# Products of weights and keys on four 32-column tiles of the array, and a new plan of the first loads

## The chip, the cores and the metric

The kernel runs on one core of a Trainium2 chip. The metric is the device time of one execution in microseconds (us); the median of several runs is compared. The core's engines are called PE (TensorE), DVE (VectorE), ACT (ScalarE), POOL (GpSimd) and SP (SyncE, which only issues transfers here).

## What is computed

Two layers, each a Fourier mixing step and a product-key mixture of experts, both with a residual:

```python
def _A_ref(x, dft_seq_re, dft_seq_im, dft_hid_re, dft_hid_im):
    a = jnp.einsum("bsd,ed->bse", x, dft_hid_re)
    b = jnp.einsum("bsd,ed->bse", x, dft_hid_im)
    return jnp.einsum("ts,bse->bte", dft_seq_re, a) - jnp.einsum("ts,bse->bte", dft_seq_im, b)

def _B_ref(x, w_q, k1, k2, u, v):          # S=2048, D=512, H=32, dk=128, E=16, K=2
    q = jnp.einsum("nd,dhc->nhc", xf, w_q)
    q1, q2 = q[..., :dk], q[..., dk:]
    s1 = jnp.einsum("nhd,ed->nhe", q1, k1)
    s2 = jnp.einsum("nhd,ed->nhe", q2, k2)
    ...  # the best 2 of each, the best 2 of their 4 sums, softmax g, experts ue and ve
    act = _gelu(jnp.einsum("nd,nhkd->nhk", xf, ue))
    return jnp.einsum("nhk,nhk,nhkd->nd", g, act, ve)

x = x + _A_ref(_layernorm(x), ...)
x = x + _B_ref(_layernorm(x), ...)
x = x + _A_ref(_layernorm(x), ...)
x = x + _B_ref(_layernorm(x), ...)
```

## The kernel before

Tokens lie in 16 row tiles `rows[:, r]` of 128 tokens by 512. The scores of a token are its row times `w_q` times the keys, so the kernel multiplies `w_q` by the keys once, at the start, and keeps the product in two f16 words, `wh` and `wl`. It also uses the symmetries of the Fourier matrices: rows that mirror each other are added and subtracted first ("folded").

The work ahead of the first row of scores is this:

- **Rows of x** (`load_x`): 7 by SP, 9 gathered by POOL. Each gets statistics on DVE (`ln_bn`), one power on POOL and a scaling on ACT.
- **Folds** (`fold`, four of them, q = 0 to 3, each of four row tiles): about ten additions of 512 columns on DVE, with small steps on POOL; the result is `eo` in two words.
- **Fourier blocks** (`load_c`, `load_edges`, and `dhid` in `setup`): loads, then splits on ACT and DVE into `cc`, `edge`, `tcol` and `dd`.
- **Weights times keys** (`setup`, `visit(f, g)`): for each of the two key matrices f and four groups g of eight heads, 2 MB of `w_q` come in four loads of 512 KB into four buffers of `wraw` (pool "wr"). `kpad` holds the 16 keys eight times along a diagonal in zeros, so that a 128-column weight of it puts head z's scores into output rows 16 z to 16 z + 15; eight f32 products of 512 columns (L1867) add up in one bank. ACT copies the bank (L1877), PE transposes it in four pieces (L1882), ACT and DVE split it into `wh` and `wl`.
- **Experts' tables**: `ut` and `vm`, split into `uh`, `ul`, `vh`, `vl`.
- **Mixing along the sequence** (`seq_pair`, L1941): `eo` times `cc`, pair by pair, then `hidden` (L2072), which adds to the rows.

Then `peers` runs for each of 16 rows in each of two layers, and `L2154` is its first product, the scores: it waits for all of `setup_done`, which holds every split of `w_q`, `ut` and `vm`. Beside the rows runs a check of the Fourier matrices' symmetry, on ACT, DVE, POOL and by loads into the buffers `raws` (pool "raw", six of 512 KB).

The order on every engine is set when the kernel is built. Each piece of work is an `op` with an engine, an assumed time, what it waits for, the buffers it takes and gives back, and a priority `prio`. `Plan.best` lays them out in time twice, the second time by due times worked out from the first, and the instructions are issued in that order. For a load the assumed time is a tuple (issue, transfer, latency), and not more than `LANES` = 8 may be under way on a queue. At issue, PE also gets products that nothing reads (`fill`, L2710) wherever the plan has it idle.

Of the kernel before, what the change touches and what calls it, by code (L numbers as in the profile page):

```python
# [17 lines left out]
P = 128  # L18
# [11 lines left out]
E = 16  # L30
# [189 lines left out]
def load(kb):  # L220
    return 0.5, kb / 256 * 0.98, 2.05
# [1175 lines left out]

class Late:
# [22 lines left out]
REPOSE, STEP = 0.25, 0.065  # L1421
EARLY = 2


@with_exitstack
def folded(ctx: ExitStack, tc, flag, x_in, cseq, ctile, dhid, wq, k1t, k2t, ut, vm, out):
# [57 lines left out]
    kpad = [spare[:, f * 1152:(f + 1) * 1152] for f in range(2)]  # L1484
# [32 lines left out]
    nc.vector.memset(spare[:, :2304], 0.0)  # L1517
# [28 lines left out]
    slots = {"wr": [0, 1, 2, 3], "ws": [0, 1], "code": [0, 1, 2], "pq": [0, 1]}  # L1546
# [73 lines left out]
    def load_x(r, turn):  # L1620
# [6 lines left out]
        xload[r] = op("SP" if place(r) else "POOL", load(256), f, prio=(-2, turn))  # L1627
        xstat[0, r] = ln_bn(lambda: rows[:, r], stats[0][:, r], FS, [xload[r]], (-4, r // 4, 0, r))
# [102 lines left out]
    def load_c(n, c, prio, low):  # L1731
# [7 lines left out]
        a = op("SP", load(512), f, take=[h], prio=low)  # L1739
# [18 lines left out]
    def load_edges():  # L1758
        h, one_ = Hold("raw"), {}

        def f0():
            for z, (n, c) in enumerate(((6, 0), (6, 1))):
                for h in range(2):
                    nc.sync.dma_start(tc32[:, z, 2 * h:2 * h + 2], cseq[n, c, 2 * h:2 * h + 2, :, 0].rearrange("i p -> (i p)").rearrange("(p a) -> p a", a=2))

        def f1():
            for p in (0, 32, 64):
                nc.sync.dma_start(one_[0][p:p + 1], cseq[0:2, 0, 4, 0:1, :].rearrange("n p t -> p n t"))
                nc.sync.dma_start(one15[p:p + 1], cseq[6, 0, 4, 0:1, 0:1])
# [28 lines left out]
        b = op("ACT", 0.6, g2, [b], prio=(-3, 20))  # L1798
# [4 lines left out]
    def setup():  # L1803
# [29 lines left out]
        a = op("SP", load(512), f, take=[hd, hd2], prio=(-1, 0))  # L1833
        b = op("SP", (0.5, 0.2, 2.0), f_mid, behind=[a], prio=(-1, 1))
# [5 lines left out]
        for f, kt in enumerate((k1t, k2t)):  # L1840
# [933 lines left out]
```

## Time and profile before

| | |
|---|---|
| Median of 3 runs | 660.16 us (659.52 to 660.43) |
| Profiled execution | 664.53 us, span 662.5 us |
| PE, busy | 559.7 us, 84% of the span |
| DVE, busy | 504.6 us, 76% |
| ACT, busy | 394.6 us, 60% |
| POOL, busy | 242.2 us, 37% |
| Granted clock of PE, mean | 0.949 |
| Moved by DMA | 88.29 MB, mean 133 GB/s |

All times in the profile are from one profiled execution, counted from its span's start. A row of the timeline has start, length, engine, line, operation, output <- input, tile of the array, shape and count; in brackets stands the idle time ahead of it and what ended it. SPq and POOLq rows are the issuing of transfers, not their moving. "issue" means that the engine waited for nothing that the profile shows.

### The profile page before, as it was taken

The numbers are of one execution on the slowest core, as the hardware profiler recorded it, in microseconds if no ns is written. First come the engines' busy times: TensorE is split into PE (matmuls) and PEld (weight loads), VectorE is DVE, ScalarE is ACT, GpSimd is POOL, SyncE is SP. The second block draws the span as 40 slices with busy tenths as digits, with TensorE's granted clock in tenths as the row PEclk, the third lists the DMA queues.
The fourth block names the chain that finished last, engine by engine and source line by source line (L and its number), as shares of the span: only waits on it lengthen the run. The fifth ranks groups of instructions, "written<-read, shape, count | busy, mean of one in ns | idle before, by whom it ended". The sixth has DMA issues, their size and how long they took to land.

```text
span 662.5 us, 17484 instructions
## 1 busy us (share of the span) xinstructions
PE 559.7 (84%) x7083; PEld 363.4 (55%) x7115; DVE 504.6 (76%) x1001; ACT 394.6 (60%) x995; POOL 242.2 (37%) x370
## 2 busy tenths in 40 slices
PE   3986899998978879888995758998979988999965
PEld 2644455654555646446554647655656555555553
DVE  3579823797798878899598434689994899889963
ACT  2148326996668866857655625947863865554450
POOL 7254000355156627315145100331723263431730
PEclk9997999998999979989997986999989999999988
DMA  8785573439656687573729230044798569795683
GB/s 306 211 294 176 162 253 128 140 57 182 96 157 119 108 183 113 97 128 49 145 49 144 31 133 1 1 97 94 106 194 144 120 101 223 137 178 130 116 169 57
DMA packets 174702, 88.29 MB, mean 133 GB/s; under 512 B 138758, under 2 KB 151570, under 8 KB 174614
## 3 DMA queue, kind: packets, MB, share of 16 engines
q1 hardware_dynamic: 161718, 52.49, 34.5%
q0 software_dynamic: 12896, 34.61, 27.4%
q8 instruction: 57, 0.93, 0.6%
q14 instruction: 31, 0.25, 0.1%
HBM read 78.68 MB, written 8.39 MB: 131 GB/s over the span
## 4 chain that ended last, share of the span: by engine, by line
PE 37%; DVE 36%; DMA 8%; ACT 8%; issue 5%; POOL 3%; SPq 2%; another core or an unknown queue 0%; POOLq 0%; DVEq 0%; ACTq 0%
PE sc L2154 13%; DVE eq L2200 6%; DVE val L2195 6%; PE bank L1867 6%; DMA gt<-gdr 5%; PE bank L2384 3%; DVE wraw L2307 3%; DVE wraw L2312 3%; PE bank L2168 3%; PE bank L2328 2%; DMA gdr<-spare 2%; PE small L2710 2%; PE small L2208 2%; PE bank L2072 2%; SPq L2345 1%
## 5 line engine op out<-in xcount | busy, mean ns | idle before, releaser
L2154 PE MATMUL sc<-wh,xt 128*128 128x512 f16 x512 | 132.9, 386 | 0.7
L2154 PEld LDWEIGHTS <-xt 128*128 128x128 f16 x768 | 74.2, 99 | 84.5 <-issue 4.7
L1597 POOL TENSOR_TENSOR stats<-stats,half 128x1 f32<-128x1 f32 x48 | 32.5, 677 | 197.9 <-ACT stats L1594 197.9
L2195 DVE TENSOR_REDUCE val<-sc 128x64 f32<-128x1024 f32 x64 | 77.8, 1218 | 22.8 <-PE sc L2154 14.8
L2444 POOL DMA_DIRECT2D raws<-in_cseq x56 | 59.0, 1080 | 56.2 <-issue 38.3
L2200 DVE TENSOR_TENSOR eq<-sc,val 128x1024 bf16<-128x1024 f32 x64 | 77.8, 1217 | 0.7
L2415 ACT ACTIVATE raws<-raws 128x1024 f32<-128x1024 f32 (+2 forms) x68 | 68.7, 1011 | 10.0 <-DVE raws L2420 7.0
L2710 PE MATMUL small<-ident 128*128 128x64 f16 x1272 | 52.6, 202 | 20.4 <-DVE small L1548 6.5
L2154 PE MATMUL sc<-wl,xt 128*128 128x512 f16 x256 | 66.9, 384 | 0.0
L2710 PEld LDWEIGHTS <-ident 128*128 128x128 f16 x1272 | 49.0, 104 | 29.9 <-issue 22.1
L1867 PE MATMUL bank<-wraw,spare 128*128 128x512 f32 x128 | 61.4, 626 | 0.0
L2334 ACT ACTIVATE spare<-bank 128x512 f32<-128x512 f32 x64 | 36.7, 595 | 32.8 <-PE bank L2328 30.7
L2208 PE MATMUL small<-eq,power 128*128 128x64 bf16 x1024 | 41.9, 196 | 16.3 <-DVE eq L2200 12.7
L2208 PEld LDWEIGHTS <-power 128*128 128x128 bf16 x1024 | 38.5, 100 | 22.4 <-issue 14.3
L2328 PE MATMUL bank<-wraw 64*64 64x64 f16 x2048 | 43.7, 198 | 7.9 <-DVE wraw L2312 2.8
L2328 PEld LDWEIGHTS <-wraw 64*64 64x64 f16 x2048 | 39.2, 114 | 19.9 <-issue 16.5
L2307 DVE TENSOR_TENSOR wraw<-places,qt 128x2048 f16<-128x2048 f16 x32 | 41.5, 1295 | 8.8 <-ACT qt L2290 8.8
L2312 DVE TENSOR_TENSOR wraw<-wraw,qt 128x1024 f16<-128x1024 f16 x64 | 43.7, 693 | 0.3
L2384 PE MATMUL bank<-vh,pp 128*128 128x512 f16 x128 | 41.3, 406 | 3.1 <-DVE pp L2371 3.0
L2168 PEld LDWEIGHTS <-xt 128*128 128x128 f16 x384 | 36.9, 98 | 9.4 <-issue 1.5
L1591 ACT ACTIVATE junk<-rows 128x512 f16<-128x512 f32 x48 | 30.0, 626 | 19.3 <-DVE rows L2388 12.0
L2168 PE MATMUL bank<-uh,xt 128*128 128x256 f16 x256 | 39.0, 276 | 1.6 <-ACT pd L1987 0.7
(235 smaller groups left out, 1108.9 us busy)
## 6 DMA issues: line engine op xcount, KB each, us to landing
raws<-in_cseq POOLq DMA_DIRECT2D x40, 512.0 KB
wraw<-in_wq SPq DMA_DIRECT2D x32, 512.0 KB
raws<-in_cseq SPq DMA_DIRECT2D x32, 512.0 KB
gdr<-spare SPq DMA_DIRECT2D x128, 32.0 KB
gt<-gdr SPq DMA_DIRECT2D x64, 64.0 KB
raws<-in_ctile SPq DMA_DIRECT2D x32, 128.0 KB
raws<-in_cseq POOLq DMA_DIRECT2D x16, 256.0 KB
rows<-in_x SPq DMA_DIRECT2D x7, 256.0 KB
```

What stands on the lines that cost most here:

```text
L1867: nc.tensor.matmul(t["b"], kpad[f][:, z * P:(z + 1) * P], t["wr", m][:, a], start=(z == 0), stop=(z == 7))
L2154: nc.tensor.matmul(t["sc"][:, f], t["x"][:, z, k], m[:, k, f], start=(n == 0), stop=False, skip_group_check=True)
L2168: nc.tensor.matmul(t["xu"], t["x"][:, z, k], m[:, k], start=(n == 0), stop=(n == 3 * KD - 1))
L2195: nc.vector.tensor_reduce(t["val"][:, k], flip(), axis=AX.X, op=ALU.max)
L2200: nc.vector.tensor_tensor(t["eq"], t["sc"], t["val"][:, k][:, :, None, :].to_broadcast([P, 2, E, H]), op=ALU.is_equal)
L2208: nc.tensor.matmul(t["code", k], power[:, e], t["eq"][:, :, e], start=(e == 0), stop=(e == E - 1), skip_group_check=True)
L2307: nc.vector.tensor_tensor(t["m"][:, 0:2].rearrange("p v g e t -> p (v g) e t"), io, both, op=ALU.is_equal)
L2312: nc.vector.tensor_mul(t["m"][:, 2 + k], t["m"][:, 1], row_of(2 + k))
L2328: nc.tensor.matmul(pg[js, g], t["m"][js, 0, 8 * z + g], t["m"][js, 2 + k, 8 * z + g], start=(k == 0), stop=(k == 1), skip_group_check=True)
L2384: nc.tensor.matmul(t["po"], t["pp"][:, z, k], m[:, k], start=(n == 0), stop=(n == 5))
L2415: nc.scalar.activation((to or src)(), src(), AF.Square, accum_out=sq[:src().shape[0], k:k + 1])
L2710: nc.tensor.matmul(small[:, 448:], ident16, ident16[:, :64], start=False, stop=True, skip_group_check=True)
```

## The change

The product of weights and keys now uses 32-column tiles of the array. `kpad` shrinks to 64 columns per key matrix: two weights of 32 columns, the keys in the first 16 columns of one and the last 16 of the other. A piece of `w_q` is four heads of equal parity by half of the columns (256), still 512 KB, in runs of 1 KB instead of 2 KB. Its four products go to output rows 32 j to 32 j + 31 for j = 0 to 3, each on column tile j; two pieces (even and odd heads) add up.

Nine of the 32 pieces (the 15th and every second one after it, counted from 0) take a buffer of `raws`, so that there are ten buffers in all. All loads of the first stage get a new assumed time, 0.70 us for 256 KB instead of 0.98, and new priorities; several small loads that were one `op` become one `op` each. The plan issues no fills before its time 45.

```diff
+def fetch(kb):
+    return 0.5, kb / 256 * 0.70, 2.05
...
+COLD = 45.0
+SHARED = range(15, 32, 2)
+def ORDER(k):
+    return 0.75 * k + WFIRST
+WFIRST = 10
...
-    kpad = [spare[:, f * 1152:(f + 1) * 1152] for f in range(2)]
+    kpad = [spare[:, f * 64:(f + 1) * 64] for f in range(2)]
...
-    nc.vector.memset(spare[:, :2304], 0.0)
+    nc.vector.memset(spare[:, :128], 0.0)
...
-        a = op("SP", (2.0, 1.7, 2.0, 4), f0, prio=(-2, 15, 4))
+        a = [op("SP", (0.5, 0.4, 2.0), f0(z, h), prio=(-2, 14.3, 1)) for z in range(2) for h in range(2)]
...
-        b = op("SP", (3.0, 0.2, 2.0, 6), f1, [b], prio=(-2, 15, 5))
+        b = [op("SP", (0.5, 0.05, 2.0), f1(p, z), [b], prio=(-2, 14.3, 2)) for p in (0, 32, 64) for z in range(2)]
...
-        a = op("SP", load(512), f, take=[hd, hd2], prio=(-1, 0))
+        a = op("SP", fetch(512), f, take=[hd, hd2], prio=(-2, 14.4))
...
-                diagonal = kpad[f].rearrange("p (h x) -> p h x", x=P + E)[:, :, :E]
-                nc.vector.tensor_copy(diagonal, kr[:, f][:, None, :].to_broadcast([P, 8, E]))
+                for a in range(2):
+                    nc.vector.tensor_copy(kpad[f][:, 3 * E * a:3 * E * a + E], kr[:, f])
...
-            for m in range(4):
-                h = Hold("wr")
+            for z in range(4):
+                k = 16 * f + 4 * g + z
+                h = Hold("raw" if k in SHARED else "wr")
...
-                    nc.sync.dma_start(t["wr", m], wq[f, 8 * g + 2 * m:8 * g + 2 * m + 2].rearrange("h c d -> c h d"))
+                    nc.sync.dma_start(t["w", z], wq[f, 8 * g + z % 2:8 * g + 8:2, :, z // 2 * T:(z // 2 + 1) * T].rearrange("h c d -> c h d"))
...
-                    for a in range(2):
-                        z = 2 * m + a
-                        nc.tensor.matmul(t["b"], kpad[f][:, z * P:(z + 1) * P], t["wr", m][:, a], start=(z == 0), stop=(z == 7))
+                    a, d = z % 2, z // 2 * T
+                    for j in range(4):
+                        nc.tensor.matmul(t["b"][32 * j:32 * j + 32, d:d + T], kpad[f][:, 32 * a:32 * a + 32], t["w", z][:, j], start=(a == 0),
+                                         stop=(a == 1), skip_group_check=True, tile_position=(0, 32 * j))
...
-                a_pe = op("PE", 2 * 0.87, f1, [a, kready[f], a_pe], take=[] if m else [hb], last=[h], prio=(-1, f, g))
+                o = op("SP", fetch(512), f0, take=[h], prio=(-2, ORDER(k)))
+                a_pe = op("PE", 0.55, f1, [o, kready[f], a_pe], take=[] if z else [hb], last=[h], prio=(-1, f, g))
...
-            a = op("SP", load(512), f0, take=[h], prio=(-1, 3, z))
+            a = op("SP", fetch(512), f0, take=[h], prio=(-2, ORDER(27), z))
...
-    idle = 0.0
+    idle = COLD
...
-            idle = o.start + o.us
+            idle = max(idle, o.start + o.us)
```

Since the plan is made anew, the order changes on every engine. Lines move too: the product L1867 becomes L1881, the sequence products L1941 become L1954, the first scores product L2154 becomes L2167, the `w_q` load L1860 becomes L1874.

SP, from the kernel's start, before (rows of x are L1623, cseq blocks L1736):

```order
L1842 DMA kr<-in_k1t 128x16
L1842 DMA kr<-in_k2t 128x16
L1860 DMA wraw<-in_wq 128x2x512 x4
L1623 DMA rows<-in_x 128x512 x3
L1736 DMA raws<-in_cseq 128x2x512 x2
L1860 DMA wraw<-in_wq 128x2x512 x4
L1623 DMA rows<-in_x 128x512 x4
```

and now (rows of x are L1635, cseq blocks L1751):

```order
L1635 DMA rows<-in_x 128x512
L1874 DMA wraw<-in_wq 128x4x256
L1856 DMA kr<-in_k1t 128x16
L1874 DMA wraw<-in_wq 128x4x256
L1635 DMA rows<-in_x 128x512
L1874 DMA wraw<-in_wq 128x4x256 x2
L1635 DMA rows<-in_x 128x512
L1751 DMA raws<-in_cseq 128x2x512 x2
L1791 DMA s_92<-in_cseq 1x2x256
L1874 DMA wraw<-in_wq 128x4x256 x2
L1635 DMA rows<-in_x 128x512
```

Rows of x and pieces of `w_q` alternate, and the second key matrix is loaded much later.

PE, at its first product of weights and keys, before (`ident` is the weight of a fill; 104 fills stand ahead of this):

```order
L1867 MATMUL bank<-wraw,spare 128x512 x2
L2710 LDWEIGHTS ident_99
L2710 MATMUL small<-ident_99 128x64
L2710 LDWEIGHTS ident_99
L2710 MATMUL small<-ident_99 128x64
L2710 LDWEIGHTS ident_99
```

and now, from the kernel's start:

```order
L1881 MATMUL bank<-wraw,spare 32x256 x16
L1895 MATMUL bank<-identf,spare 128x128 x4
L1881 MATMUL bank<-wraw,spare 32x256 x16
L1895 MATMUL bank<-identf,spare 128x128 x4
L1881 MATMUL bank<-wraw,spare 32x256 x8
L1954 LDWEIGHTS eo
L1954 MATMUL sc<-cc,eo 128x128
```

Sixteen products are four pieces, one visit; ten pieces stand ahead of the first sequence product, where eleven loads of `w_q` stood before, and the fills are gone from here.

DVE, at the copies of the keys (`kr` to `spare`, which holds `kpad`), before:

```order
L1773 MEMSET raws 65x512
L1774 MEMSET one_83 65x1
L1846 COPY spare<-kr 128x8x16 x2
L1576 BN_STATS bn<-rows 128x6
L1579 BN_AGGR stats_103<-bn 128x2
```

and now, first at the copies of the first key matrix, then at those of the second:

```order
L1588 BN_STATS bn<-rows 128x6 x2
L1591 BN_AGGR stats_103<-bn 128x2 x2
L1592 TENSOR_SCALAR stats_103<-stats_103 128x1 x2
L1595 SCALAR_TENSOR_TENSOR stats_103<-stats_103 128x1
L1860 COPY spare<-kr 128x16 x2
L1588 BN_STATS bn<-rows 128x6
```

```order
L1718 TENSOR_TENSOR fabs<-fabs 128x2x2x128
L1700 TENSOR_TENSOR fabs<-fabs 128x2x255
L1721 TENSOR_TENSOR fabs<-fabs 128x2x256
L1703 COPY fabs<-fabs 128x2
L1860 COPY spare<-kr 128x16 x2
L1712 TENSOR_SCALAR fabs<-fabs 128x2x2
L1766 SCALAR_TENSOR_TENSOR cc<-raws,cc 128x512
```

Both copies stood ahead of all statistics; now the first stands behind the statistics of two rows, and the second among the last two folds.

More of the change, by code (lines that the diff above doesn't have):

```diff
@@ L1544, in raw @@
         return m
-    slots = {"wr": [0, 1, 2, 3], "ws": [0, 1], "code": [0, 1, 2], "pq": [0, 1]}
+    slots = {"ws": [0, 1], "code": [0, 1, 2], "pq": [0, 1]}
     small = psum.tile([P, 512], F32, name="small", bufs=1)
@@ L1625, in f @@
                 gather(rows[:, r], x_in, turned(r))
-        xload[r] = op("SP" if place(r) else "POOL", load(256), f, prio=(-2, turn))
-        xstat[0, r] = ln_bn(lambda: rows[:, r], stats[0][:, r], FS, [xload[r]], (-4, r // 4, 0, r))
+        xload[r] = op("SP" if place(r) else "POOL", fetch(256), f, prio=(-2, turn))
+        if r % 4 in BYACT:
+            xstat[0, r] = ln_sums(lambda: rows[:, r], stats[0][:, r], sums[:, r], FS, [xload[r]], (-4, r // 4, 0, r))
+        else:
+            xstat[0, r] = ln_bn(lambda: rows[:, r], stats[0][:, r], FS, [xload[r]], (-4, r // 4, 0, r))
     eo_free = {}
@@ L1737, in f @@
                               cseq[n, c, 0:4].rearrange("i p t -> (i p) t").rearrange("(h p a) t -> p h (a t)", h=2, a=2))
-        a = op("SP", load(512), f, take=[h], prio=low)
+        a = op("SP", fetch(512), f, take=[h], prio=low)
         if c:
@@ L1759, in load_edges, with f0, f1 @@
         h, one_ = Hold("raw"), {}
[L1761 to L1769, printed above, removed]
+        def f0(z, h):
+            return lambda: nc.sync.dma_start(tc32[:, z, 2 * h:2 * h + 2],
+                                             cseq[6, z, 2 * h:2 * h + 2, :, 0].rearrange("i p -> (i p)").rearrange("(p a) -> p a", a=2))
+        def f1(p, z):
+            if z:
+                return lambda: nc.sync.dma_start(one15[p:p + 1], cseq[6, 0, 4, 0:1, 0:1])
+            return lambda: nc.sync.dma_start(one_[0][p:p + 1], cseq[0:2, 0, 4, 0:1, :].rearrange("n p t -> p n t"))
         def f2():
@@ L1796, in g3 @@
                 nc.vector.scalar_tensor_tensor(dst, src, CS, dst, op0=ALU.mult, op1=ALU.subtract)
-        b = op("ACT", 0.6, g2, [b], prio=(-3, 20))
+        b = op("ACT", 0.6, g2, b, prio=(-3, 20))
         e_ready.append(op("DVE", 0.8, g3, [b], last=[h], prio=(-3, 20)))
@@ L1831, in f1 @@
             nc.vector.scalar_tensor_tensor(dd[:, 1, 3], parts(1, 1), -DS, dd[:, 0, 3], op0=ALU.mult, op1=ALU.subtract)
-        a = op("SP", load(512), f, take=[hd, hd2], prio=(-1, 0))
-        b = op("SP", (0.5, 0.2, 2.0), f_mid, behind=[a], prio=(-1, 1))
+        a = op("SP", fetch(512), f, take=[hd, hd2], prio=(-2, 14.4))
+        b = op("SP", (0.5, 0.2, 2.0), f_mid, behind=[a], prio=(-2, 14.45))
         a = op("POOL", 1.0, f_put, [a, b], last=[hd2], prio=(-2, 0))
@@ L2581, in check @@
             h3 = Hold("raw")
-            a = op("SP", load(512), f0, done, take=h + [h3], behind=gate(0.9), prio=(9, 8, c))
+            a = op("SP", fetch(512), f0, done, take=h + [h3], behind=gate(0.9), prio=(9, 8, c))
             def f3(w=w, c=c, h3=h3):
```

17 lines of the change are left out of this document (7 added, 10 removed).

## The prediction, made before the changed kernel was run

> **What bounds the kernel now.** I read the profile by stage first, because the change touches only the work ahead of the first scores product (L2154). The table by stage has, after the times, busy time and instructions of PE, its weight loads, DVE, ACT and POOL, then the granted clock, the share of the 16 DMA engines and GB/s.
>
> ```profile
> 0.00:20.00 20.00, 8.24 (x106) 6.42 (x107) 8.19 (x30) 4.79 (x18) 13.81 (x56) 1.00 0.86 316
> 20.00:55.00 35.00, 29.84 (x333) 17.85 (x332) 25.39 (x69) 14.01 (x23) 14.31 (x34) 1.00 0.77 241
> 55.00:75.00 20.00, 14.62 (x126) 9.15 (x126) 19.43 (x42) 12.97 (x22) 6.23 (x19) 0.83 0.55 159
> 75.00:114.00 39.00, 38.74 (x195) 20.87 (x192) 13.78 (x27) 15.48 (x41) 0.74 (x2) 1.00 0.57 190
> 114.00:662.50 548.50, 468.23 (x6332) 309.16 (x6362) 437.79 (x837) 347.36 (x893) 207.10 (x259) 0.94 0.61 115
> ```
>
> Up to 114 us three things take turns: loads (0 to 20), the fold chain on DVE (55 to 75: 19.4 of 20 us) and PE (75 to 114: 38.7 of 39 us). The last 548.5 us are the token rows, which keep their code. So the question is when the first L2154 can start. Now PE in order of time:
>
> ```profile
> 18.93 3.29 PE L1867 MATMUL bank<-wraw,spare 128*128 128x512 f32 x4
> ...
> 58.41 0.59 PE L1941 MATMUL sc<-cc,eo 128*128 128x128 f16 x4 [3.83 <-DVE stats L1580]
> ...
> 87.72 7.03 PE L1867 MATMUL bank<-wraw,spare 128*128 128x512 f32 x16
> 94.59 0.60 PE L1882 MATMUL bank<-identf,spare 128*128 128x128 f32 x4
> 95.03 0.17 PE L1951 MATMUL small<-eo,cc 128*128 128x2 f16 x1
> ...
> 112.12 0.60 PE L2130 MATMUL bank<-identf,xn 128*128 128x128 f32 x4
> ...
> 114.06 1.04 PE L2154 MATMUL sc<-wh,xt 128*128 128x512 f16 x4
> ```
>
> At 58.41 PE has waited 3.8 us for the fold chain. Sixteen records of L1867 fill 87.72 to 94.59, 0.43 us each; an f32 product leaves two, so one 512 KB load of w_q (two products) costs 1.72 us, and the 32 of them 55 us. The queue of loads shows the rest:
>
> ```profile
> 5.19 1.00 SPq L1736 DMA_DIRECT2D raws<-in_cseq  x2
> 22.25 6.99 SPq L1860 DMA_DIRECT2D wraw<-in_wq  x4
> ...
> 59.23 0.37 SPq L1910 DMA_DIRECT2D raws<-in_ut  x1
> 61.76 0.37 SPq L1910 DMA_DIRECT2D raws<-in_vm  x1
> 62.55 8.43 SPq L1860 DMA_DIRECT2D wraw<-in_wq  x4
> 71.03 2.60 SPq L1764 DMA_DIRECT2D tc<-in_cseq  x4
> ...
> 91.52 12.11 SPq L1860 DMA_DIRECT2D wraw<-in_wq  x7
> ```
>
> SP stands from 6.2 to 22.25 until the first of four buffers is read, and at the end issues seven loads in 12.1 us, 1.73 us each: PE's pace, with the DMA engines at 0.57.
>
> **The change, part by part.**
>
> *The product on column tiles.* Each load (still 512 KB) gives four f32 products of 256 columns on 32-column tiles, so eight records of 0.43 / 2 = 0.215 us: 1.72 us if they go one after another, 0.43 us if all four tiles run together. No row has 32-column tiles. The nearest has two 64×64 tiles that share neither rows nor columns:
>
> ```profile
> 140.88 0.60 PE L2168 MATMUL bank<-uh,xt 128*128 128x256 f16 x4
> 141.41 1.20 PE L2328 MATMUL bank<-wraw 64*64 64x64 f16 x64
> 142.54 0.64 PE L2208 MATMUL small<-eq,power 128*128 128x64 bf16 x16
> ```
>
> With 0.19 us taken off for the last one's own length, 64 tiled products step by 16 ns and 16 full ones of the same 64 columns by 30 ns: 1.9 times, nearly the two that two tiles allow. So tiles do run together here. By that factor a load costs 0.9 us, by four tiles 0.43; I take 0.9 and keep 0.43 and 1.72 as ends. Anything under the transfers' pace (1.37 us, below) gives the same sum, since PE then waits for loads: 55 us of PE become at most 29. The Trainium skill (TensorE: Matmul & The Clock Gate, Part 3) gives measured speedups of 2.38 for three column tiles and 3.07 for four row tiles; an estimate from the latter is 1.72 / 3.07 = 0.56 us, and the sum would stay what it is. No row here shows column tiles alone.
>
> *Loads.* Ahead of the first L2154 stand 32 pieces of w_q, 16 rows of x (7 from SP, 9 gathered by POOL), 4 blocks of cseq, and dhid, ut and vm, 512 KB each: 24.6 MB. The run of bytes in a w_q piece falls from 2 KB to 1 KB (256 f32). The load of ut has 1 KB runs, and from 61.50 was alone in flight; 64.00 to 64.25 has 2 KB runs:
>
> ```profile
> 61.50:61.75 0.25, 0.25 (x2) 0.11 (x1) 0.25 (x2) 0.25 (x2) 0.00 (x0) 0.50 1.09 389
> 64.00:64.25 0.25, 0.25 (x8) 0.25 (x6) 0.25 (x2) 0.25 (x2) 0.00 (x0) 1.00 1.03 401
> ...
> wraw<-in_wq SPq DMA_DIRECT2D x32, 512.0 KB
> ...
> rows<-in_x SPq DMA_DIRECT2D x7, 256.0 KB
> ```
>
> 389 against 401 GB/s: short runs cost 3%. I use 385, 1.37 us a piece; all bytes take 64 us. That is a floor of about 66 for the last load and 71 for the first L2154.
>
> *Smaller edits.* The 2304-wide memset of `spare` (DVE 4.37 to 6.35) goes, but DVE then waits for x (row at 11.01 below), so nothing is gained by it alone. The diagonal copies become two 16-wide copies per key matrix, at most the 0.24 us they were. The fills before 45 us of plan time go: nobody waits for a fill, but the first products then run at the half clock. The bound is twice 0.9 us for four pieces, 4 us from 12.6 to 20, in which loads are still arriving. Split small loads keep their number.
>
> *Fold chain.* DVE's rows:
>
> ```profile
> 11.01 0.69 DVE L1576 BATCH_NORM_STATS2 bn<-rows 128x6 f32<-128x512 f32 x1 [3.66 <-DMA rows<-in_x,turns]
> ...
> 42.55 0.70 DVE L1676 TENSOR_TENSOR fabs<-fabs 128x513 f32<-128x513 f32 x1 [3.06 <-POOL fabs L1661]
> 43.16 0.69 DVE L1648 TENSOR_TENSOR fabs<-fabs 128x512 f32<-128x512 f32 x1
> ...
> 53.27 2.49 DVE L1560 SCALAR_TENSOR_TENSOR eo<-fabs,eo 128x514 f16<-128x514 f32 x4
> ...
> 74.75 1.22 DVE L1560 SCALAR_TENSOR_TENSOR ul<-raws,uh 128x1024 f16<-128x1024 f32 x1
> ...
> 79.49 1.30 DVE L1560 SCALAR_TENSOR_TENSOR eo<-fabs,eo 128x514 f16<-128x514 f32 x2 [0.78 <-ACT eo L1557]
> ...
> 101.55 0.69 DVE L2081 SCALAR_TENSOR_TENSOR rows<-bank,rows 128x512 f32<-128x512 f32 x1 [1.52 <-PE bank L2072]
> ```
>
> Two 512-wide instructions start 0.61 us apart (42.55, 43.16). In the new order the key copy stands behind the statistics of a gathered row, which lands at 11.0: the first w_q product starts near 12.6, not 18.9. The last SP row of x lands when 9.4 MB are through, 2 + 9.4 / 0.385 = 26.5 (its issue now follows the wait until 22.25). From there to the fourth `eo` of the first two folds the order has 26 such instructions (15.9 us) and small ones (1.4): 44, with 2 us for stalls 46, against 55.8 now. The last two folds' `eo` follow after 27 more (16.5), the dhid split and small ones (3.8), with 3 us for stalls: 69, against 80.8 now.
>
> *What that does to the loads.* PE's order has 10 pieces ahead of the first L1954 (L1941 before), which waits for those `eo` at 46. Four more fit into `wraw`; the order of SP then stands. Through the 14th piece 13.6 MB are moved, at about 37 to 39. So the DMA engines idle from 39 to 49. The 18 pieces left, one cseq block, ut and vm are 11.0 MB: 28.6 us; the small loads between them cost issue time (four took 2.6 us), 3 us; the last landing 2 us: 82.6. Then one 1024-wide split on ACT and one on DVE (1.04 and 1.22 at ul): 85.
>
> *The tail of the row chain.* From the last `eo` at 69, L1954 takes 0.7. Then now, with PE otherwise full:
>
> ```profile
> 73.00 1.04 ACT L1557 ACTIVATE uh<-raws 128x1024 f16<-128x1024 f32 x1
> ...
> 105.25 0.81 ACT L1604 ACTIVATE xn<-rows,stats 128x512 f32<-128x512 f32 x1 [0.45 <-POOL stats L1598]
> ```
>
> From L1951 at 95.03 to the end of that xn at 106.06 are 11.0 us, and from L2130 at 112.12 to L2154 at 114.06 1.9. Before, 6.1 us between them were PE's queue of w_q products, which is gone; ACT's uh and vh splits and one w_q visit now stand among these, 3 us. 69.7 + 11.0 + 1.9 + 3 = 85.6.
>
> *The sum.* Loads give 85, the row chain 86; two chains of like length end later than either, so I take 87 for the first L2154: 114 - 87 = 27 us. The 548.5 us behind it I leave as they are: the new order has 36 products of the next pair (2 us) and one hidden product (1.3 us) ahead of the first L2154, which would take 3 off, and every row there is planned anew, which can cost as much; ends -3 and +5. The profiled execution took 664.53 us with a span of 662.5; it becomes 637.5. The median of the runs lies 4.4 lower: 633.
>
> **The rivals.**
>
> *Folds later (DVE is the bound).* If DVE stalls as it did before 42.55 (3.1 us for POOL's part of the first fold) four times over instead of 5 us in all, both chains move by 7 to 10: first L2154 at 95, 641.
>
> *Loads never stand.* If the first `eo` come before 40, the 10 us of idle DMA go, and the fold chain follows: 77, 623.
>
> *The tiles do not run together.* 22 pieces are left behind the first `eo`: 37.8 us at 1.72, beside 15 us of other products: 46 + 53 + 2.5 for the last split = 101; gain 13, 647. Against it: the 64×64 row.
>
> *Slower: instructions arrive late behind the loads.*
>
> ```profile
> 10.11 0.45 PE L2710 MATMUL small<-ident 128*128 128x64 f16 x5 [0.39 <-issue]
> 11.55 0.39 PE L2710 MATMUL small<-ident 128*128 128x64 f16 x4 [0.99 <-issue]
> ...
> 17.25 1.87 PE L2710 MATMUL small<-ident 128*128 128x64 f16 x32 [0.49 <-issue]
> ...
> 12.00:14.00 2.00, 0.53 (x4) 0.20 (x3) 0.81 (x2) 0.00 (x0) 1.59 (x2) 1.00 1.03 379
> 46.00:48.00 2.00, 2.00 (x6) 0.84 (x5) 2.00 (x4) 0.00 (x0) 1.04 (x1) 1.00 1.04 399
> ```
>
> Between 9.7 and 17.3 PE sat idle 5.2 us in nine gaps of 0.4 to 1.0 with nothing to wait for but its own issue (the first two and the last are shown), while the DMA engines were full. The change keeps them full longer. Six such episodes on the path cost 31 us and turn the gain into 664; it decides from a little over five. Against it: from 46 to 48 they were as full and PE had no gap. The Trainium skill (Runtime: NRT & Kernel Launch, Instruction fetch mechanics) holds that the fetch of instructions is mostly hidden; by that rule this rival falls away, but the gap ahead of 11.55 doesn't look hidden.
>
> *Short runs are slow in company.* If 1 KB pieces moved at 230 GB/s, the 16.8 MB of w_q would take 73 us, the rest 20, and the stall 10: first L2154 at 108, 654. Against it: 389 above.
>
> **How the numbers follow.** 0.50 for my sum with its own range (627 to 638), 0.22 for late folds (638 to 647), 0.13 for loads that never stand (617 to 627), 0.07 for tiles in series, 0.03 for slow short runs, 0.04 for late instructions, 0.01 for no change. 619 to 648 leaves out the last of these and the ends of the others, under 2 in 10. What counts as no change is 0.2% (1.3 us), about what a measurement of this kernel can tell. Only late instructions are slower: 0.04; same 0.01; faster 0.95.
>
> **What would show it.** Right: the first scores product at 84 to 90; the w_q records of one load within 1 us; the DMA engines at 0.9 or more up to about 38, a hole of some 10 us that PE spends waiting for `eo`, and full again to about 80; 545 to 553 us from the first scores product to the end. Wrong: w_q pieces 1.7 us apart on PE with SP paced by them (series); DMA share full but under 300 GB/s (short runs); gaps on PE put down to issue (instructions); a tail of rows that differs by more than 5 us, which would say that the new plan reaches further than the first stage.

## The result, and the profile after

The changed kernel takes 638.72 us, median of 4 runs (634.2 to 643.79), where the kernel before took 659.89 (659.52 to 660.43) beside it: a ratio of 0.9656, 95% interval 0.9589 to 0.9722. Medians are over all runs of a kernel, ratios and their intervals leave out those that took over 1.5% longer than its fastest. The profiled execution took 641.07 us with a span of 639.3 us. Against the span of before, 662.5, that is 23.2 us less.

The table by stage of the changed kernel, with the columns of the one shown before:

```profile
0.00:20.00 20.00, 3.23 (x32) 1.37 (x32) 6.67 (x32) 7.22 (x21) 15.33 (x60) 1.00 0.93 324
20.00:40.00 20.00, 6.96 (x56) 3.28 (x56) 19.51 (x50) 9.19 (x15) 12.42 (x27) 0.65 1.03 342
40.00:50.00 10.00, 6.88 (x80) 5.12 (x84) 10.00 (x35) 6.14 (x12) 5.10 (x10) 0.68 0.27 91
50.00:60.00 10.00, 6.30 (x95) 4.66 (x88) 8.70 (x18) 8.38 (x17) 2.49 (x9) 0.67 0.94 283
60.00:80.00 20.00, 17.50 (x272) 12.15 (x269) 14.07 (x33) 9.29 (x25) 0.73 (x1) 0.91 1.10 349
80.00:90.26 10.26, 8.62 (x131) 7.00 (x128) 6.56 (x11) 8.54 (x20) 1.27 (x6) 1.00 0.48 178
90.26:639.30 549.04, 465.51 (x6347) 305.61 (x6375) 434.44 (x830) 345.40 (x888) 208.35 (x259) 0.94 0.61 114
```

The whole difference lies in the first stage. The first scores product starts at 90.26 instead of 114.06, and what follows takes 549.0 us instead of 548.5. PE, which was full from 75 to 114 us, is now busy for 17.5 of the 20 us from 60 to 80. From 20 to 50 us DVE is the engine that is full (19.5 of 20, then 10 of 10); from 50 to 60 it is busy for 8.7 of 10.

PE in order of time:

```profile
16.50 3.23 PE L1881 MATMUL bank<-wraw,spare 128*32 128x256 f32 x32 [16.50 <-DVE spare L1860]
...
42.99 2.64 PE L1954 MATMUL sc<-cc,eo 128*128 128x128 f16 x23 [1.26 <-DVE eo L1572]
...
64.29 1.15 PE L1881 MATMUL bank<-raws,spare 128*32 128x256 f32 x8
65.14 1.15 PE L1881 MATMUL bank<-wraw,spare 128*32 128x256 f32 x8
...
72.64 0.64 PE L1881 MATMUL bank<-wraw,spare 128*32 128x256 f32 x8
73.10 0.61 PE L1881 MATMUL bank<-raws,spare 128*32 128x256 f32 x8
...
81.33 0.64 PE L1881 MATMUL bank<-wraw,spare 128*32 128x256 f32 x8 [1.18 <-DMA wraw<-in_wq]
81.78 0.61 PE L1881 MATMUL bank<-raws,spare 128*32 128x256 f32 x8
...
86.18 0.64 PE L2143 MATMUL bank<-identf,xn 128*128 128x128 f32 x4
...
88.91 1.51 PE L1954 MATMUL bank<-cc,eo 128*128 128x128 f16 x24 [0.46 <-DVE wl L1908]
90.26 1.03 PE L2167 MATMUL sc<-wh,xt 128*128 128x512 f16 x4
```

One piece is eight records. Two pieces in a row start 0.46 us apart at full clock (72.64, 73.10; granted clock 1.00 from 72.6 to 73.5) and 0.85 apart at half clock (64.29, 65.14; 0.50 from 64 to 66.5); before, a load of the same size took 1.72. The last piece is done at 82.4, and 7.9 us pass until the first scores product. SP's queue:

```profile
37.03 10.03 SPq L1874 DMA_DIRECT2D wraw<-in_wq  x2
...
58.92 4.50 SPq L1874 DMA_DIRECT2D raws<-in_wq  x2
...
75.68 1.37 SPq L1923 DMA_DIRECT2D raws<-in_vm  x1
```

and DVE at the last `eo` of the first two folds, the copy of the second key matrix and the last `eo` of all:

```profile
46.19 1.28 DVE L1572 SCALAR_TENSOR_TENSOR eo<-fabs,eo 128x514 f16<-128x514 f32 x2
...
63.23 0.24 DVE L1860 COPY spare<-kr 128x16 f32<-128x16 f32 x2
...
68.33 1.30 DVE L1572 SCALAR_TENSOR_TENSOR eo<-fabs,eo 128x514 f16<-128x514 f32 x2 [0.57 <-ACT eo L1569]
```

SP stands for 10 us at 37.0, while PE has its products of w_q behind the wait for the first folds, and again at 58.9, while the second key matrix is not yet copied (63.23).

### The profile page after: what moved, and what is told of

Read it like the earlier page. It is cut to its first block, busy times and chain, and to the rows that moved or that the text cites. A ratio compares the mean times of both kernels' runs of the same rounds, so it can differ in the third digit from the quotient of the medians.

```text
span 639.3 us, 17351 instructions
## 1 busy us (share of the span) xinstructions
PE 515.0 (81%) x6993; PEld 339.2 (53%) x7024; DVE 499.9 (78%) x1003; ACT 394.2 (62%) x995; POOL 245.7 (38%) x370
## 4 chain that ended last, share of the span: by engine, by line
DVE 32%; PE 27%; ACT 15%; DMA 13%; issue 7%; SPq 3%; POOL 2%; POOLq 0%; ACTq 0%; DVEq 0%
PE sc L2167 9%; DMA gt<-gdr 8%; DVE eq L2213 6%; DVE val L2208 6%; PE bank L2397 3%; PE bank L2181 3%; ACT junk L1605 3%; DMA gdr<-spare 3%; DVE wraw L2320 2%; SPq L2358 2%; DVE wraw L2325 2%; ACT junk L1603 2%; PE small L2221 2%; PE bank L2085 2%; ACT raws L2428 2%
## 5 line engine op out<-in xcount | busy, mean ns | idle before, releaser
L2167 PE MATMUL sc<-wh,xt 128*128 128x512 f16 x512 | 132.4, 386 | 0.6
L2167 PEld LDWEIGHTS <-xt 128*128 128x128 f16 x768 | 74.5, 99 | 86.6 <-issue 6.5
L2428 ACT ACTIVATE raws<-raws 128x1024 f32<-128x1024 f32 (+3 forms) x68 | 68.7, 1011 | 6.1 <-DVE raws L2433 4.0
L2167 PE MATMUL sc<-wl,xt 128*128 128x512 f16 x256 | 68.1, 390 | 0.0
L2723 PE MATMUL small<-ident 128*128 128x64 f16 x1053 | 42.5, 203 | 5.5 <-DVE q L2231 3.1
L2723 PEld LDWEIGHTS <-ident 128*128 128x128 f16 x1053 | 40.8, 105 | 10.0 <-issue 8.2
L2341 PEld LDWEIGHTS <-wraw 64*64 64x64 f16 x2048 | 37.8, 112 | 13.6 <-issue 10.8
L2320 DVE TENSOR_TENSOR wraw<-places,qt 128x2048 f16<-128x2048 f16 x32 | 39.0, 1218 | 4.3 <-ACT qt L2303 4.3
L2381 ACT ACTIVATE pp<-bank 128x256 f16<-128x256 f32 x32 | 12.1, 378 | 41.8 <-PE bank L2377 41.8
```

What stands on the lines that cost most here:

```text
L2167: nc.tensor.matmul(t["sc"][:, f], t["x"][:, z, k], m[:, k, f], start=(n == 0), stop=False, skip_group_check=True)
L2320: nc.vector.tensor_tensor(t["m"][:, 0:2].rearrange("p v g e t -> p (v g) e t"), io, both, op=ALU.is_equal)
L2341: nc.tensor.matmul(pg[js, g], t["m"][js, 0, 8 * z + g], t["m"][js, 2 + k, 8 * z + g], start=(k == 0), stop=(k == 1), skip_group_check=True)
L2428: nc.scalar.activation((to or src)(), src(), AF.Square, accum_out=sq[:src().shape[0], k:k + 1])
L2723: nc.tensor.matmul(small[:, 448:], ident16, ident16[:, :64], start=False, stop=True, skip_group_check=True)
```

## Experiments

Two theories stood against each other. *Loads*: the stage ends when the last loads have landed and been used; column tiles take PE off them. *Rows*: it ends with the chain from the last `eo` over the sequence products, the hidden rows, their statistics and transposes to the first scores product; the rest only has to stay out of its way. Beside that, the change has several parts (tiles with 1 KB runs, early edge loads, assumed transfer times, order numbers of the loads, ten buffers, no early fills), and it was open which of them carry the 24 us.

Each comparison has its own runs of the kernel before, with medians of 658.3 to 666.2 us on the chips used, so ratios are compared across experiments, and places in the first stage, which hardly moved: the same program a second time gave 90.03 for 90.26.

### The changed kernel again

> The changed kernel itself, once more, to see how much its time moves from run to run (its four runs lay between 634.2 and 643.8 us, those of the kernel before between 659.5 and 660.4). If the spread comes from the first stage, the first scores product starts at another time than 90.3 us and the rest stays near 549 us; if it comes from the token rows, the first stage ends at 90 again and the rest differs by some us. I expect 634 to 644 us, the first stage ending at 89 to 91, and the difference in the rows behind it.

Median 639.3 us of 4 runs (631.51 to 641.61), beside 666.07 for before; the two medians give 0.960, its two shorter runs (631.51 and 637.46) against the median of before 0.953. So the ratio of one and the same program moves by about a hundredth from one series to the next. Its profiled span is 635.7 us with the first scores product at 90.03, so 3.4 of the 3.6 us between the two profiles lie in the token rows (545.7 and 549.0), as expected.

### Column tiles alone

The kernel before, with only the product changed, and with it `kpad` and the cut of `w_q` into pieces:

```
-  nc.tensor.matmul(t["b"], kpad[f][:, z * P:(z + 1) * P], t["wr", m][:, a], ...)
+  for j in range(4):
+      nc.tensor.matmul(t["b"][32 * j:32 * j + 32, d:d + T], kpad[f][:, 32 * a:32 * a + 32],
+                       t["wr", m][:, j], ..., tile_position=(0, 32 * j))
-  a_pe = op("PE", 2 * 0.87, f1, ...)
+  a_pe = op("PE", 0.55, f1, ...)
```

> The kernel before with the products on column tiles alone: its four buffers, its assumed times of 0.98 us per 256 KB and its priorities stay. If the tiles carry the gain (PE bounded the stage from 75 to 114 us), the products take about 0.45 us a piece instead of 1.72, loads and folds set the pace, and the first scores product starts at 88 to 95: 637 to 644 us. If the plan of the loads carries it, the start stays above 105: over 652 us.

673.3 us, ratio 1.0101 (1.0047 to 1.0156): slower by 1%. The first scores product starts at 121.13, 7 us later than before. SP of this kernel:

```profile
67.82 26.26 SPq L1860 DMA_DIRECT2D wraw<-in_wq  x13
94.13 0.64 SPq L1768 DMA_DIRECT2D raws<-in_cseq  x1
```

and its PE, from the last two pieces on:

```profile
98.12 0.67 PE L2711 MATMUL small<-ident 128*128 128x64 f16 x17
100.46 0.64 PE L1867 MATMUL bank<-wraw,spare 128*32 128x256 f32 x8 [1.68 <-DMA wraw<-in_wq]
...
102.61 0.27 PE L1960 MATMUL sc<-edge,xe 65*128 65x128 f16 x2
...
107.34 2.63 PE L2073 MATMUL bank<-dd,p 128*128 128x256 f16 x12
```

The row of a piece lasts 0.64 us, where a load held PE for 1.72, and PE fills the time won with filling products (L2711). The edge loads stand behind the last w_q load on SP (94.13), so the edge products come at 102.6, behind the last w_q product; before, they ran at 95.3 with w_q products still to come. From there to the scores product are 18.5 us; before, the same way took 18.8 (95.26 to 114.06), with w_q products beside it. So the loss of 7 us is the later start of the edge products. In these 18.5 us ACT is busy for 17.2 and PE for 17.0, fills included. I had not expected a loss.

### All of the change but the tiles

The changed kernel with the full-array products, 2 KB runs and their 1.74 us in the plan.

> The changed kernel with the old products (eight of 512 columns on the full array, 1.72 us for 512 KB, runs of 2 KB) in the new plan: ten buffers, the new assumed times and priorities, and no fills early on. If the tiles carry the gain, PE has 55 us of these products again and the first scores product starts at 105 to 112: 652 to 659 us. If the plan and the buffers carry it, it starts below 97: under 645 us.

667.8 us, ratio 1.0028 (0.9992 to 1.0064): no gain, at the place that was expected and with a longer time. PE runs 18 pieces in a row, with only their transposes between them, and the row chain starts behind them:

```profile
58.70 1.98 PE L1881 MATMUL bank<-wraw,spare 128*128 128x512 f32 x4 [0.75 <-DMA wraw<-in_wq]
...
89.74 1.88 PE L1881 MATMUL bank<-raws,spare 128*128 128x512 f32 x4
91.46 1.50 PE L1953 MATMUL sc<-cc,eo 128*128 128x128 f16 x24
```

Its last `eo` was ready at 81.8; PE reaches the products that read it at 91.46, and the first scores product follows 20.1 us later, at 111.58. So neither the tiles nor the rest wins anything by itself.

### Runs of 2 KB on two tiles

```
-  wq[f, 8 * g + z % 2:8 * g + 8:2, :, z // 2 * T:(z // 2 + 1) * T]     (4 heads x 256)
+  wq[f, x:x + 3:2]          with x = 8 * g + 4 * (z // 2) + z % 2      (2 heads x 512)
```

> The changed kernel with pieces of two heads by 512 columns (runs of 2 KB) instead of four heads by 256 (1 KB); two column tiles at a time instead of four, so that a piece takes 0.86 us on PE. Between 60 and 80 us the transfers ran at 347 to 350 GB/s with 1 KB runs. If the short runs are the reason, they run at 380 to 400 here, the last piece lands 5 us earlier than 81.3, and the first scores product starts at 85 to 87: 3 to 5 us faster than the changed kernel. If the rate has another reason (several transfers at once), it stays below 360 and the time within 1.5 us of the changed kernel's.

643.34 us, ratio 0.9657 (0.9585 to 0.9729), as the changed kernel (whose second series, on the same chip, took 639.3 us). The first scores product starts at 91.51. The row from 60 to 80 us of this kernel, to be read beside that of the changed one above:

```profile
60.00:80.00 20.00, 16.52 (x152) 7.96 (x153) 13.37 (x31) 7.10 (x14) 0.73 (x1) 0.91 1.01 363
```

363 GB/s instead of 349, with the DMA engines at 1.01 instead of 1.10, a difference of 4%. But this is a mean over stretches that differ. With runs of 2 KB the trace shows 387 GB/s from 60 to 66 us and 396 from 74 to 78, both at a share of 1.05, and 317 from 68 to 74, where the share is 0.94. With runs of 1 KB it is 347 to 350 in all of them, at 1.09 or 1.10. Where the queue keeps the engines full, pieces in runs of 1 KB are thus some 10% slower, and the first half of the theory holds. These pieces also skip every second KB of `w_q`; no run tells that from the length of the runs. The last w_q product still starts at 82.60 (81.78 in the changed kernel), so the higher rate gained nothing.

### Tiles and early edge loads

Column tiles alone, and beside them only the split edge loads, the `s512` row and dhid at the places of the changed kernel (`prio=(-2, 14.3, ...)`, `(-2, 5.5)`, `(-2, 14.4)`).

> Edit: the kernel with column tiles alone (first scores product at 121.1, last w_q product at 100.5), and beside it only the loads of the edge elements (split into single transfers) and of dhid with the early places they have in the changed kernel; the transfer times of the plan and the four buffers stay those of before. Theory (the tiles alone lose because the edge loads still stand behind all w_q loads on SP, so the chain from the edge products to xn runs alone for 18.5 us after the w_q products): the edge products come ahead of the last w_q product, the chain runs beside the w_q products, first scores product at 101 to 107, time about 655 (0.985 of before). Rival (the four buffers and the old transfer times set the pace, the edges don't matter): first scores product still at 115 to 122, time 667 to 674, ratio 1.00 to 1.01.

656.2 us, ratio 0.9823 (0.9737 to 0.9909); the first scores product starts at 109.91. The time is the theory's, the place is 3 us beyond its range: 11.2 of the 121.1 us went with the earlier loads of edges and dhid. What ends the stage here is the last w_q product, at 104.0, with PE's visits and 36 products of the next pair behind it.

### Tiles, early edge loads and new transfer times

```
+def fetch(kb):
+    return 0.5, kb / 256 * 0.70, 2.05
-  a = op("SP", load(512), f0, take=[h], ...)
+  a = op("SP", fetch(512), f0, take=[h], ...)
```

> Edit: the kernel with tiles and early edge loads (first scores product at 109.9) and beside it the new transfer times alone (0.70 us for 256 KB); four buffers, the order numbers of the w_q loads and the fills stay those of before. Theory (the assumed times are what was still missing): last w_q product at 85 to 92 instead of 104.0, first scores product at 91 to 98, time 640 to 646, ratio 0.965. Rival (the order numbers of the w_q loads are needed, since with those of before nine w_q loads stand behind vm): first scores product at 100 to 110, time 648 to 657.

648.59 us, ratio 0.9737 (0.9643 to 0.983). Its profiled execution took 652.24 us, above that median. In it the last w_q product starts at 83.88, a little ahead of the theory's range, and the first scores product at 96.27, within it: another 13.6 us. The median lies at the lower end of the rival's range (648), two of the four runs (641.15 and 644.93) in the theory's, so the places decide here and not the time.

### The changed kernel with the old transfer times

> Edit: the changed kernel with the transfer times that the plan assumed before (0.98 us for 256 KB instead of 0.70); tiles, places of the loads, ten buffers as changed. Theory (the assumed times do it: with 1.96 us for a piece the plan puts other work of PE between two pieces, so that SP waits for buffers and the last pieces come late): first scores product at 98 to 106, time 648 to 655, ratio 0.975 to 0.985. Rival (the places of the loads and the buffers do it, the assumed times only shift the plan's own clock): first scores product at 89 to 93, time 639 to 643, ratio 0.966.

659.96 us, ratio 0.9993 (0.9958 to 1.0028). The whole gain is gone, more than the theory expected. SP of this kernel, and PE:

```profile
30.03 16.55 SPq L1874 DMA_DIRECT2D wraw<-in_wq  x3
...
70.89 12.98 SPq L1874 DMA_DIRECT2D wraw<-in_wq  x5
```

```profile
24.64 1.08 PE L1881 MATMUL bank<-wraw,spare 128*32 128x256 f32 x8 [1.12 <-DMA wraw<-in_wq]
44.05 1.09 PE L1895 MATMUL bank<-identf,spare 128*128 128x128 f32 x4 [18.33 <-ACT spare L1890]
...
107.61 0.64 PE L1881 MATMUL bank<-raws,spare 128*32 128x256 f32 x8
```

With 1.96 us for a piece the plan puts x and the edge loads first, and has PE transpose the first visit where the pieces are planned to have come. That transpose waits for a copy of ACT's that stands behind the folds (18.33 us at 44.05), the four buffers stay full, and SP stands for 16.5 us. The last folds are early (`eo` to 67.3), but the last w_q product starts at 107.61, and the stage ends at 111.54. The assumed time does its work through the order that the plan makes of it.

### Four buffers

`SHARED = ()` in the changed kernel.

> Edit: the changed kernel with all w_q pieces in the four buffers of before (none in the shared ones). Theory (the loads are bound by the transfer rate and by the wait for the first folds, PE reads each piece in 0.45 us, so four buffers feed it nearly as well): last w_q product and first scores product within 4 us of the changed kernel's 90, time 637 to 643, ratio 0.966. Rival (ten buffers are what lets SP run ahead): SP waits for buffers through 50 to 80 us, DMA share under 0.8 there, first scores product at 97 to 104, time 646 to 653, ratio 0.975 to 0.985.

643.84 us, ratio 0.9662 (0.9589 to 0.9735); first scores product at 90.81. The last w_q product moves from 81.78 to 86.48, and the first scores product by 0.5. The ten buffers carry none of the gain that these runs can tell.

### Second key matrix early

```
-  a_pe = op("PE", 0.55, f1, [o, kready[f], a_pe], ...)
+  a_pe = op("PE", 0.55, f1, [o, kready[f], kready[1 - f], a_pe], ...)
```

> Edit: the changed kernel, but the first w_q product waits for the copies of both key matrices, so that the second one is loaded and copied at the start (before, its copy ran on DVE at 63.2 and PE had no w_q product from 54.1 to 63.5, SP stood 3.5 us for buffers at 58.9). Theory (the loads end the stage): those 3.5 us and some of PE's queue go, last w_q product at 78 instead of 81.8, first scores product at 86 to 88, time 636 (ratio 0.961). Rival (the chain of the rows from the last fold's eo at 69.6 ends the stage, loads have slack): first scores product at 89 to 91, time as the changed kernel's 639 to 643, ratio 0.966.

639.49 us, ratio 0.9595 (0.9509 to 0.9682): not to be told from the changed kernel. The last `eo` ends at 66.1 (69.6), the last w_q product starts at 81.11 (81.78), the first scores product at 88.96 (90.26). The place lies between the two expectations. SP's one long wait at 58.9 becomes several of 1.8 to 2.8 us from 54.8 on, and the loads end only 0.7 us earlier. The folds end 3.5 us earlier, of which 1.3 arrive at the scores product; that they bring it is likely, but this run doesn't show it.

### The same without the hole in the loads

```
-  first = [] if i else ... early[layer, b - 1] if b >= EARLY else []
+  first = [] if i else ... early[layer, b - 1] if b >= EARLY else [pieces[13]]
```

> Edit: as the kernel with early keys, and the first products of the folded rows (L1954) stand behind the 14th w_q piece on PE, not the 10th or 11th, so that buffers come free while the first folds are still awaited (SP stood 10 us at 37.0 in the changed kernel). Theory: the hole of the DMA engines at 39 to 47 shrinks to 3 us or less, all loads land by 74, and the chain of the rows from the last eo (69.6) alone ends the stage: first scores product at 84 to 87, time 633 to 636 (ratio 0.957). Rival (earlier loads slow the folds, or DVE is late with the splits that the loads wait for): last eo later than 71, first scores product 88 or later, no gain over the kernel with early keys alone.

642.52 us, ratio 0.9629 (0.9558 to 0.9699). This run tells the two theories apart. Two stretches of its table by stage, and PE at the last w_q product and at the first scores product:

```profile
40.00:50.00 10.00, 4.92 (x36) 1.16 (x34) 9.94 (x23) 4.63 (x11) 3.97 (x6) 1.00 0.77 243
...
80.00:90.00 10.00, 8.36 (x144) 7.73 (x145) 6.62 (x13) 9.72 (x29) 2.01 (x8) 1.00 0.01 2
```

```profile
75.66 0.61 PE L1882 MATMUL bank<-raws,spare 128*32 128x256 f32 x8
...
90.85 1.04 PE L2169 MATMUL sc<-wh,xt 128*128 128x512 f16 x4 [0.18 <-ACT xt L2149]
```

The hole from 40 to 50 us is mostly filled (share 0.77 for 0.27), the loads are through before 80, and the last w_q product starts 6 us earlier. The first scores product stays at 90.85. So loads that end 6 us earlier, with the folds where they were in the changed kernel, win nothing, and *loads* falls as the cause of the stage's length. My number for the rows was wrong too: with the last `eo` at 69.1 I gave 84 to 87, and what came is the rival's "88 or later, no gain", though not by its later folds. From 80 to 90 us the DMA engines move almost nothing (share 0.01), and ACT is busy for 9.7 of 10 us: it has another split and a second row's statistics ahead of the first xn (87.08), and a third row's statistics (88.29 to 90.3) ahead of the copy of xt at 90.23, for which PE waits. So behind the last `eo` it is ACT's queue that the row chain stands in. No run here gives ACT less to do at that place.

### Statistics of four rows on ACT

`BYACT = (1,)` in the kernel without the hole: 3.6 us less for DVE.

> Edit: the kernel with early keys and without the hole (its loads had landed by 78, its last eo came at 69.1, its first scores product at 90.9), and the statistics of four of the 16 first rows are made on ACT instead of DVE: about 4 x 0.9 = 3.6 us off DVE, which was busy for 38 of the 40 us from 30 to 70. Theory (the chain of the rows behind DVE's folds ends the first stage, the loads have slack): last eo at 65 to 66.5, first scores product at 86 to 88.5, time 636 to 639 (ratio 0.956 to 0.960). Rival (the folds wait for POOL or ACT as much as for DVE, or what is behind the last eo waits for splits of ut, vm and w_q): last eo or first scores product within 1.5 us of that kernel's, time 641 to 645.

647.13 us, ratio 0.9775 (0.9666 to 0.9884). The last `eo` ends at 68.74 instead of 69.11, the first scores product starts at 89.70 instead of 90.85: the rival's places; the time lies above both expectations. DVE, with 3.6 us less to do, is busy for 7.9 of the 10 us from 60 to 70 instead of all 10, so the folds wait for others by then, and the 21 us behind them stay. That a shorter fold chain shortens the stage is therefore not shown by this run.

### Fills back

`COLD = 0.0` in the changed kernel.

> Edit: the changed kernel with the filling products of PE before 45 us of plan time put back (the only part of the change not yet taken apart; without them PE ran at half clock for 99.9 us of the changed kernel, 69.7 us of the one before). Theory (products in the first 45 us wait for loads and folds, so their pace costs nothing, and the first stage ends by the chain of the rows behind the last fold): first scores product at 89 to 92, time 637 to 643 (ratio 0.966 on a chip like the first). Rival 1 (the half clock delays the first w_q visits and through them loads and folds): first scores product at 84 to 88, time 3 to 6 us lower. Rival 2 (filling products stand ahead of w_q products on PE and hold back buffers): first scores product at 93 to 97, as in the kernel with tiles, early edge loads and new transfer times, which has these fills, and ended its stage at 96.3.

633.75 us (632.15 to 635.24), ratio 0.9613 (0.9542 to 0.9684), an interval that shares most of its length with the changed kernel's. The first scores product starts at 89.69, as the theory says; the time is 3 us below its range, and in the profile those lie behind the first stage (543.7 us, 549.0 in the changed kernel). From 20 to 40 us the mean granted clock is 0.91 instead of 0.65. What PE does there waits for loads and folds either way.

### What the runs say together

| kernel | last `eo` ends | last w_q product starts | first scores product | ratio of times |
|---|---|---|---|---|
| before | 80.8 | 108.7 | 114.06 | 1 |
| tiles alone | 78.8 | 100.46 | 121.13 | 1.010 |
| + early edge loads | 75.4 | 104.04 | 109.91 | 0.982 |
| + transfer times | 73.7 | 83.88 | 96.27 | 0.974 |
| changed, four buffers | 69.3 | 86.48 | 90.81 | 0.966 |
| changed | 69.6 | 81.78 | 90.26 | 0.966 |
| changed, old transfer times | 67.3 | 107.61 | 111.54 | 0.999 |
| changed, full-array products | 81.8 | 89.74 | 111.58 | 1.003 |
| changed, 2 KB runs | 69.5 | 82.60 | 91.51 | 0.966 |
| keys early | 66.1 | 81.11 | 88.96 | 0.960 |
| keys early, no hole | 69.1 | 75.66 | 90.85 | 0.963 |
| the same, statistics on ACT | 68.7 | 73.87 | 89.70 | 0.978 |
| fills back | 68.7 | 81.22 | 89.69 | 0.961 |

In every kernel whose last w_q product starts by 86.5, the first scores product stands 20.6 to 22.8 us behind the last `eo`. The step from the third rung to the fourth (5.5 us) is not taken apart further than to the order numbers of the loads and the fills, and the fills moved nothing in the changed kernel. No version tried can be told from the changed kernel on the better side.

## Why the prediction was right, point by point

*The bound and the sum.* I gave 87 for the first scores product, out of two chains of 85 and 86, and 549 for the rest; it is 90.26 and 549.0. The place is just beyond the 84 to 90 that I named as a sign of being right, and the median, 638.7, is 5.7 us above my 633 and just beyond the sum's own range of 627 to 638; it lies within the whole range, 619 to 648. Of the 5.7 us, 3.3 are the later first scores product and 0.5 the rest. About 2 come from the median of the runs, which I put 4.4 us under the profiled execution as before; it is 2.4 under it.

*The product on column tiles.* Taken as 0.9 us a piece, ends 0.43 and 1.72; measured 0.46 at full clock, so nearly the end where all four tiles run together; on two tiles, in the kernel with 2 KB runs, pieces start 0.88 us apart. By the Trainium skill (TensorE: Matmul & The Clock Gate, Part 3) it would have been an estimated 0.56 (from the 3.07 for four row tiles); the trace shows a factor of 1.72 / 0.46 = 3.7 for four column tiles in f32. As said, the sum didn't hang on it. The rival of tiles in series falls.

*Transfer rate.* Mis-sized by 2.9 us: 385 GB/s, taken from a load alone in flight, against 349 with the queue full from 60 to 80 us. The 11.0 MB behind the stall take 31.5 us by it, not 28.6. I had the cost of short runs right for one load (3%) and carried it over to a full queue, where the kernel with 2 KB runs shows 387 to 396 and w_q's pieces in runs of 1 KB 347 to 350, some 10% less. The rival of short runs that lose in company had this mechanism with a much larger price. That the transfers fall off from 83.5 us on, near my 82.6 for the last landing, is in part luck: SP went on at 47.06 and not at 49.

*The hole.* Predicted 39 to 49, ten pieces ahead of the wait, then four buffers; measured 10.03 us of SP at 37.0 and a share of 0.27 from 40 to 50. Right, and it cost nothing, as the kernel without it shows.

*Folds.* 46 and 69 predicted, 47.5 and 69.6 measured.

*First product.* 12.6 predicted, 16.5 measured. The key copy on DVE waits behind a statistics step that needs POOL, and POOL issues its nine gathers first. POOL, then DVE:

```profile
14.60 0.95 POOL L1576 DMA_INDIRECT rows<-in_x,turns  x1 [0.31 <-issue]
15.57 1.11 POOL L1594 TENSOR_TENSOR stats<-stats,half 128x1 f32<-128x1 f32 x2
```

```profile
16.20 0.16 DVE L1595 SCALAR_TENSOR_TENSOR stats<-stats 128x1 f32<-128x1 f32 x1 [3.59 <-POOL stats L1594]
16.28 0.24 DVE L1860 COPY spare<-kr 128x16 f32<-128x16 f32 x2
```

I followed DVE's order to the row's landing and left out POOL's queue. It cost nothing that the trace shows, since the DMA engines were full until then (share 1.05, 382 GB/s from 8 to 16.5 us).

*The tail of the row chain.* The step that was mis-sized most: 16.6 us from the last `eo` (69.0 to 85.6), of which 3 for other work in the queues; measured 20.6. Nearly all of the 4.0 us lie behind xn: from its end to the first scores product I took 1.9 us from before, and it is 5.6 (84.71 to 90.26). The chain runs over engines that each have other work ahead of the chain's step. ACT of the changed kernel:

```profile
79.73 0.56 ACT L1905 CAST wh<-bank 128x512 f16<-128x512 f32 x1
...
80.30 0.62 ACT L1603 ACTIVATE junk<-rows 128x512 f16<-128x512 f32 x1
...
83.91 0.80 ACT L1616 ACTIVATE xn<-rows,stats 128x512 f32<-128x512 f32 x1
...
87.08 1.07 ACT L1569 ACTIVATE vh<-raws 128x1024 f16<-128x1024 f32 x1
88.04 0.59 ACT L2147 CAST xt<-bank 128x512 f16<-128x512 f32 x1
```

and DVE, at the hidden row and at the last splits:

```profile
78.75 0.69 DVE L2094 SCALAR_TENSOR_TENSOR rows<-bank,rows 128x512 f32<-128x512 f32 x1 [0.96 <-PE bank L2085]
...
88.17 0.68 DVE L1908 TENSOR_TENSOR wl<-bank,wh 128x512 f16<-128x512 f32 x1
...
89.36 1.22 DVE L1572 SCALAR_TENSOR_TENSOR vl<-raws,vh 128x1024 f16<-128x1024 f32 x1
```

The hidden row is ready at 79.44 and ACT takes it at 80.30; POOL has the statistics at 83.22 (L1610) and ACT makes xn at 83.91, behind a split; xn ends at 84.71 and PE transposes it at 86.18; that ends at 86.82 and ACT copies it at 88.04, behind vh; the copy ends at 88.63 and PE, with 36 products of the next pair ahead, begins the scores at 90.26. That is 0.9 + 0.7 + 1.5 + 1.2 + 1.6 = 5.9 us of detours, the hand-overs between engines included. I named two splits and one visit, and had put the 36 products down as a gain behind the first stage; they stand in the chain.

*Two chains of like length.* Half right. In the changed kernel they meet on PE: the chain of waits, followed back from 92 us, goes from ACT's copy of xt over vh, wh and pd on ACT (86.13 to 88.16) and the 24 products of the hidden rows at 82.4 to the last pieces and their loads.

```profile
72.16 9.13 DMA wraw<-in_wq
...
81.33 1.07 PE bank L1881 x16
82.40 2.73 PE bank L2085 x24
```

So several of the five short waits are behind work that the loads bring: the pieces' products on PE, the splits on ACT, and at the end the split of the last visit, whose end at 88.85 PE waits for (0.46 us ahead of 88.91) before 24 of the 36 products. The split of vm, which I had put at the end of the loads' chain, is not on the way: `vl` ends at 90.58, behind the start of the scores product, so the wait for all of `setup_done` is one of the plan and not of this product. Yet with the loads 6 us earlier the rows' work in ACT's queue takes as much. The last step of my sum, one us for "later than either", hid a part of what the rows lacked.

*The rivals.* Late folds, loads that never stand, tiles in series and 1 KB pieces at 230 GB/s give 95, 77, 101 and 108 for the first scores product, none of which came. By the time alone, 638.7 us would fall to late folds, for which I had given 638 to 647; but the folds came at 69.6 for 69. Late instructions: up to the first scores product PE has one gap put down to its own issue, 2.17 us ahead of 63.50, and that ends with the key copy of 63.23 on DVE; the kernel with early keys lost that wait. The nine gaps of before stood between fills, which the changed kernel doesn't have at that place; what made them stays open. *Slower* was not near for the change as a whole; the tiles by themselves are slower, a case that I had no rival for, because I costed the parts one after another and not what each is worth without the others.

*The tail of rows.* 545 to 553 us predicted; 549.0 and 545.7 in two profiles of the same program, 543.7 to 556.6 over all kernels tried, though the code of the rows is the same. So the tail moves by as much as most of the variants differ in time, which is why their places are compared here; what moves it stays open.

## What to carry to other kernels

A faster instruction on a scheduled kernel is worth what the order lets it be: tiles alone lost 1%, the new plan alone won nothing, together they won 3.4%. So price a change of speed together with the order that is planned for it, and an assumed time in a planner as if it were code. Before putting two chains at the same length, follow the one step by step through every queue it passes: here five short waits of 0.7 to 1.6 us in the queues of ACT and PE, hand-overs included, made 5.9 us, where 3 had been allowed, and loads that ended 6 us earlier won nothing, since other work in ACT's queue took their place.

## What was not expected of the hardware

Four 32-column tiles with f32 operands ran together almost in full: 0.46 us for what took 1.72, and 0.85 at half clock; two of them took 0.88. A full queue moved 347 to 350 GB/s with w_q's pieces in runs of 1 KB and 387 to 396 in runs of 2 KB, at shares of the DMA engines of 1.10 and 1.05, where one load with 1 KB runs alone had shown 389 at 1.09. The share of busy time is higher at the lower rate, so it doesn't tell how near the transfers are to what they can do.
